# Batch 1's state exponentials transposed through memory and on VectorE instead of on TensorE, in a fused cross-attention and feed-forward kernel

## The chip, the cores and the metric

The kernel runs on one core of a Trainium2 chip. Its metric is the time of one execution on the device, in microseconds (us); the median of the runs shown is used. All data are 32-bit floats. "PE" is TensorE, "DVE" VectorE, "ACT" ScalarE, "SP" SyncE, whose queue issues nearly all of the DMAs here.

## The reference, cut to what matters

The input x is (B, H, S, D) = (8, 8, 512, 64), the state (8, 8, 32, 64). Tokens read the state and the state reads the tokens; the results of both, per batch 512 + 32 rows of 512 numbers, go through a feed-forward block.

```python
scores = scale * np.matmul(x, state.transpose(0, 1, 3, 2))
scores = scores - scores.max(-1, keepdims=True)
a = np.exp(scores)
a /= a.sum(-1, keepdims=True) + 1e-09
xread = np.matmul(a, state)
scores2 = scale * np.matmul(state, x.transpose(0, 1, 3, 2))
scores2 = scores2 - scores2.max(-1, keepdims=True)
a2 = np.exp(scores2)
a2 /= a2.sum(-1, keepdims=True) + 1e-09
sread = np.matmul(a2, x)
attn_out = np.concatenate([xread, sread], axis=2)
...
x = attn_out.transpose(0, 2, 1, 3).reshape(B * S, H * D)    # 4352 x 512
h = x @ w_in                                                # 512 x 2048
g = h * (1.0 / (1.0 + np.exp(-1.702 * h)))
return g @ w_out                                            # 2048 x 512
```

The weights come as 64-bit floats and are rounded to 32 bits on the chip.

## The kernel before, in words

The kernel is one program written out by hand: `tc.manual_schedule()` keeps each engine's instructions in the order of the source, and only the semaphores between engines are derived from which tile is read and written. So the place of a call in the source is its place in every queue that it touches, SP's included.

**Weights.** The 32 pieces of `PIECES` (16 of w_in, then 16 of w_out, one row block of 128 each) are loaded by `load_weight` (L199, 512 KB each) into rooms that are used in turn: a w_out piece i lies in the part i % 4 of the tile `later`, so its load waits until piece i - 4 has been rounded. Rounding a piece takes VectorE's mask (L221), then the clamp of its exponent (`round_a`), the fraction (L239), the sign (L245) and two combining steps (L258, L264). `round_a` puts the clamp on ScalarE as two activations (L232, L233), except for pieces 18 and 19 (`NFC * NPR + 2` and `+ 3`), where two VectorE instructions do it (L229, L230). `done["b"]` counts rounded pieces; `refill` issues loads after each; `rounds(n, ahead)` and `round_to` round further pieces, `powers_to(n)` does masks and clamps up to piece n.

**Batches 0 and 1** are treated first and together, while the weights arrive. Their token reads go through `M = w_in` times state (`att_M`) and then `up_x` or `up_late`, the hidden activations (PE at L655, the activation at L644, held back in a list and released by `gelus`). Their state reads go thus: `two_s_max` (L463), `two_s_exp` (eight exponentials over both batches at L474, into one tile `room`), `two_s_norm` (the inverse sums, L481 and L482), `att_eT` (L608 and L609), which turns the exponentials by 128 x 128 transposes on PE into PSUM and copies them on ScalarE to the tile `eT`, and `att_sread` (L622), 64 small matmuls of eT with the tokens, which lie with four neighbouring rows side by side.

**Batches 2 to 7** turn their exponentials otherwise: `att_s_exp` (L508) writes them in another order, `eT_out` (L588) writes them to the DRAM tile `squares` by four DMAs of 128 KB, `eT_in` (L594) reads that back as one DMA of 512 KB, and `eT_turn` (L598) transposes 32 x 32 blocks on VectorE, in place.

**Down projection of batch 0.** It is a seven-product scheme with sums of the operands (P1 to P7 in `pair`, L1539), run over eight pairs i of row blocks; for pair 0 the state reads of batches 1 and 0, `att_M(1, 2)`, `att_M(1, 3)` and an early `up_x` of batch 1 stand between P1 and P2. `left_sums` and `pair_sums` are the operand sums on VectorE (L1469). The order of the stretch in question is that of the source from `up_late(2 * nper + 1)` to the end of the branch `if i == 0` in the loop over HF.

Of the kernel before, what the change touches and what calls it, by code (L numbers as in the profile page):

```python
# [10 lines left out]
FP32 = mybir.dt.float32  # L11
I32 = mybir.dt.int32
U32 = mybir.dt.uint32
AF = mybir.ActivationFunctionType
# [6 lines left out]
def kernel(  # L21
# [36 lines left out]
    P = 128  # L58
# [157 lines left out]
    def mask(i):  # L216

        _, hi = words(i)
        sc = low[:, 2 + i % (AHEAD + 1)].bitcast(I32)
        power[i] = sc  # L220
        nc.vector.tensor_scalar(sc, hi, 0x7FF00000, None, ALU.bitwise_and)  # L221

    def round_a(i):

        if i not in power:
            mask(i)
        sc = power[i]
        if i in (NFC * NPR + 2, NFC * NPR + 3):
            nc.vector.tensor_scalar(sc, sc, most, least, ALU.min, ALU.max)  # L229
            nc.vector.tensor_scalar(sc, sc, -least, 8.0, ALU.add, ALU.mult)  # L230
            return
        nc.scalar.activation(out=sc.bitcast(FP32), in_=sc, func=AF.Relu, bias=edge[0], scale=-8.0)  # L232
        nc.scalar.activation(out=sc, in_=sc.bitcast(FP32), func=AF.Relu, bias=edge[1], scale=-1.0)  # L233
# [233 lines left out]
    def two_s_exp(b, room):  # L467
        a = A[b]
        sm = a["sm2"] = apool.tile([P, NG, 2], FP32, tag="sm4", name=f"sm4_{b}", bufs=2)
        a["e2"] = [(room[:, g], sm[:, g, :1]) for g in range(NG)]  # L470
        for g in range(NG):
            dst = room[:, g].rearrange("p (k i q) -> p k i q", k=2, i=2)
            for i in range(2):
                nc.scalar.activation(  # L474
                    out=dst[:, :, i], in_=a["s"][i][:, 2 * P * g : 2 * P * (g + 1)].rearrange("p (k q) -> p k q", k=2), func=AF.Exp,
                    bias=a["mx2"][:, 0, g : g + 1], scale=scale, accum_out=sm[:, g, i : i + 1],
                )

    def two_s_norm(b):
        sm = A[b]["sm2"]  # L480
        nc.vector.scalar_tensor_tensor(sm[:, :, 0], sm[:, :, 0], eps, sm[:, :, 1], ALU.add, ALU.add)  # L481
        nc.vector.reciprocal(out=sm[:, :, 0], in_=sm[:, :, 0])  # L482
# [12 lines left out]
    def att_s_exp(b, room=None):  # L495
        a = A[b]
        if room is None:
            room = e2_room[b] = apool.tile([P, NPR, S], FP32, tag="xT", name=f"e2_{b}")
        a["e2"] = []
        for g in range(NG):  # L500
            e = room[:, g]
            sm = apool.tile([P, 1], FP32, tag="sm2", name=f"sm2_{b}_{g}", bufs=4)
            out, src = e, a["s"][g]
            if b > 1:

                out = e.rearrange("p (i c a) -> p i a c", i=SCH, c=SCH)
                src = src.rearrange("p (i a c) -> p i a c", i=SCH, c=SCH)
            nc.scalar.activation(out=out, in_=src, func=AF.Exp, bias=a["mx2"][g], scale=scale, accum_out=sm)  # L508
            a["e2"].append((e, sm))
# [58 lines left out]
    def att_M(b, c, spare=False, banks=None, copied=True):  # L568

        m = mpool.tile([P, NG, FC], FP32, tag=f"M{turns['M'] % NFC if b < 2 else c}", name=f"M_{b}_{c}")  # L570
        turns["M"] += 1
        A[b]["M", c] = m
        name = f"M_{b}_{c}_"
        ps = banks or [
            psH.tile([P, FC], FP32, tag="h", name=name + str(g)) if spare else att_ps([P, FC], name + str(g)) for g in range(NG)
        ]
        by_state(b, ps, lambda rows, j: w_in[c][rows, j])
        M_banks[b, c] = ps
        if copied:
            M_copies(b, c)  # L580
# [3 lines left out]

    def eT_out(b):
        for j in range(NPR):
            src = e2_room[b][Ns * j : Ns * (j + 1), :NG].rearrange("n g (i q) -> n g i q", i=SCH)
            nc.sync.dma_start(squares[:, :, :, j].rearrange("i n g q -> n g i q"), src)  # L588

    def eT_in(b):  # L590

        a = A[b]
        a["eT"] = apool.tile([P, NG, SCH, P], FP32, tag="eT", name=f"eT_{b}")
        nc.sync.dma_start(a["eT"].rearrange("p g j q -> p (g j q)"), squares.rearrange("i n g j q -> (i n) (g j q)"))  # L594

    def eT_turn(b, g):
# [3 lines left out]
    def att_eT(b, g, spare=False):  # L600

        a = A[b]
        if g == 0:
            a["eT"] = apool.tile([P, NG, SCH, P], FP32, tag="e1" if b else "eT", name=f"eT_{b}")
        name = f"eT_{b}_{g}"
        ps = psH.tile([P, SCH, P], FP32, tag="h", name=name) if spare else att_ps([P, SCH, P], name)
        for c in range(SCH):
            nc.tensor.transpose(ps[:, c], a["e2"][g][0][:, P * c : P * (c + 1)], ident)  # L608
        nc.scalar.copy(a["eT"][:, g], ps)  # L609

    def att_sread(b):

        a = A[b]
        ps = att_ps([P, NG, D], f"sr_{b}")
        for g in range(NG):
            for c in range(SCH):
                for j in range(NPR):
                    st = slice(Ns * j, Ns * (j + 1))
                    e, v = a["eT"][:, g, c, st], xn[b][:, NG * j + g, c]
                    if b > 1:  # L620
                        e = a["eT"][:, g, j, Ns * c : Ns * (c + 1)]
                    nc.tensor.matmul(  # L622
                        ps[st, g], e, v,
                        start=(c == 0), stop=(c == SCH - 1),
                    )
        sr = apool.tile([P, P], FP32, tag="sr", name=f"sr_{b}", bufs=2)
        for g in range(NG):
            nc.scalar.activation(out=sr[:, D * g : D * (g + 1)], in_=ps[:, g], func=AF.Copy, scale=a["e2"][g][1])
        A[b]["sr"] = sr
# [11 lines left out]
    def gelus(n):  # L641
        for _ in range(n):
            fn, kw = waiting.pop(0)
            fn(**kw)  # L644
# [646 lines left out]
    def rounds(n, *ahead):  # L1291
        round_to(done["b"] + n, *ahead)
# [120 lines left out]
    def up_late(f, wait=True):  # L1413
        up_x(0, f, bank=late_banks[f - 2 * nper - 1], wait=wait)

    up_late(2 * nper + 1)
    att_M(0, 3)
    two_s_exp(1, room[:, NG:])
    two_s_max(0)
    up_late(2 * nper + 2)  # L1420
    two_s_exp(0, room[:, :NG])
    up_late(2 * nper + 3)
    up_late(3 * nper)
    rounds(3)
    for b in (1, 0):
        two_s_norm(b)
    up_late(3 * nper + 1)
    gelus(3)
    for g in range(NG):
        att_eT(1, g)  # L1430
    gelus(2)
    up_late(3 * nper + 2, False)
    up_late(3 * nper + 3, False)
    for g in range(NG):
        att_eT(0, g, True)


    B11, B12, B21, B22 = (w_out[:, HF * i : HF * (i + 1), HN * k : HN * (k + 1)] for i in range(2) for k in range(2))
# [22 lines left out]
    def pieces(t, *shape):  # L1461
        n, k = shape
        return t.rearrange("p a b -> p (a b)").rearrange("p (n k t) -> p n k t", n=n, k=k)
# [7 lines left out]
    def four(t):  # L1471
        return t.rearrange("p a b -> p (a b)").rearrange("p (n t) -> p n t", t=HS)
# [80 lines left out]
    for i in range(HF):  # L1553
        round_to(nin + 2 * i + 2)
        gelus(len(waiting))
        if i == 3:
            nc.scalar.copy(G[1, f_early // 2][:, f_early % 2], early)
        if i == 0:
            pair(i, "P1")
            att_sread(1)  # L1560
            att_M(1, 2, banks=bank_o[1::2])
            att_sread(0)
            att_M(1, 3, True)
            pair(i, "P2")
            f_early = rest.pop(0)
            early = xn[0].rearrange("p h c d -> p (h c d)")[:, :S]
            up_x(1, f_early, dst=early)
            att_srT(0)
            att_srT(1)
            t_room.append(pieces(apool.tile([P, NG, SCH * P], FP32, tag="eT", name="t_room_1"), 2, 2))  # L1570
            s_rooms.append(four(apool.tile([P, NG, NB * Ns], FP32, tag="e1", name="s4_room")))
            pair_sums(i)
            round_to(nin + 4)
            powers_to(nin + 6)
            pair(i, "P6")
            ps7["P7"], ps7["P3"] = (psH.tile([P, FC], FP32, tag="h", name=f"down_{k}") for k in (7, 3))
            ps7["P4"], up_bank = (att_ps([P, FC], f"down_{k}") for k in (4, "up"))
        else:
            pair_sums(i)
            pair(i, "P1", "P2")  # L1580
        if i == 2:
            G[1, f_early // 2] = free.pop(0)
        if i > 1 and i % 2 == 0:
            up_x(1, rest.pop(0), bank=up_bank, wait=True)
        if i == HF - 1:
            k1 = s_rooms[0][:, :2]
            nc.scalar.copy(k1, ps7["P1"].rearrange("p (r n) -> p r n", r=2))
        late()
        if i > 1 and i % 2:
            up_x(1, rest.pop(0), bank=up_bank if i < HF - 1 else bank_o[0], wait=True)  # L1590
        if i == HF // 2 + 1:
            load_state(2)
            load_x_squares(2)
# [140 lines left out]
```

## Time and profile before

| | |
|---|---|
| median of three runs | 689.23 us (688.90 to 689.25) |
| the profiled execution | 688.99 us, of which the span from first to last instruction is 687.2 |
| granted TensorE clock, mean | 0.998 |
| PE busy | 677.6 us, 5355 matmuls |
| DVE busy | 558.0 us, 1066 instructions |
| ACT busy | 327.9 us, 725 instructions |
| transposes of batches 0 and 1 on PE (L608) | 16 matmuls, 2.1 us |
| block transposes on DVE (L598) | 12, median 702 ns |
| DMAs on SP's queue (q1) | 86.40 MB, 42.6% of 16 engines' span |

The profile is of one execution. Its page gives busy times, the chain of work that ended last (followed back from the last instruction), the costliest groups and the DMA issues. The trace behind it gives, for any stretch, a timeline of each engine with start and length of each instruction in us, and in brackets how long the engine was idle before it and what it waited for. The ends of matmuls are modelled and overlap their successors; distances between starts tell the pace.

### The profile page before, as it was taken

Reading aid. Unit: us, or ns where it says so; the run is one execution under the profiler, and the core shown is the slowest. Engines: PE = TensorE matmul, PEld = TensorE weight load, DVE = VectorE, ACT = ScalarE, POOL = GpSimd, SP = SyncE. Lnnn points to the kernel's source line nnn. Section 1 sums busy time; section 2 is a strip of 40 time slices with the busy share of each in tenths; the row PEclk is TensorE's granted clock in tenths of the full one; section 3 lists DMA queues with packets and bytes.
Section 4 is the critical chain, followed back from the end, with each engine's and each line's share of the span. In section 5 each row is a group of like instructions: output and inputs, shape, how many; then the busy total and the mean of one; then the engine's idle time right before and its main releaser. Section 6 shows DMA issues by size and latency. Waiting matters only on the chain.

```text
span 687.2 us, 13616 instructions
## 1 busy us (share of the span) xinstructions
PE 677.6 (99%) x5355; PEld 578.7 (84%) x5355; DVE 558.0 (81%) x1066; ACT 327.9 (48%) x725; POOL 1.5 (0%) x10
## 2 busy tenths in 40 slices
PE   8999999999999999999999999999999999999996
PEld 4443687769989999889988998899988998999995
DVE  6999899999998886988878796888698885986540
ACT  7799744134355533752375335544375237421410
POOL 0000000000000000000000000000000000000000
PEclk9999999999999999999999999999999999999999
DMA  9731245338262764156443745176415640251000
GB/s 318 302 105 49 93 140 147 116 119 270 89 156 78 208 192 113 32 166 190 151 67 112 205 144 113 32 208 192 115 27 170 187 152 1 77 169 47 2 3 29
DMA packets 100159, 87.39 MB, mean 127 GB/s; under 512 B 56576, under 2 KB 79616, under 8 KB 100096
## 3 DMA queue, kind: packets, MB, share of 16 engines
q1 hardware_dynamic: 99552, 86.40, 42.6%
q8 instruction: 42, 0.69, 0.4%
q10 hardware_dynamic: 544, 0.13, 0.1%
q14 instruction: 21, 0.17, 0.1%
HBM read 68.94 MB, written 17.56 MB: 126 GB/s over the span
## 4 chain that ended last, share of the span: by engine, by line
PE 94%; DMA 2%; DVE 2%; ACT 1%; issue 0%; DVEq 0%; ACTq 0%
PE low L802 28%; PE o L1212 15%; PE o L802 15%; PE upx L1212 6%; PE o L1539 4%; PE M L430 4%; PE down L1539 3%; PE o L655 3%; PE h L655 3%; PE o L701 3%; PE upw L1212 2%; PE o L851 2%; PE down_up L655 1%; PE o L430 1%; PE sr L622 1%; PE upx_sr L1212 1%
## 5 line engine op out<-in xcount | busy, mean ns | idle before, releaser
L802 PE MATMUL low<-w_out,g_room 128*128 128x128 f32 x416 | 54.3, 276 | 0.0
L802 PEld LDWEIGHTS low<-w_out,g_room 128*128 128x128 f32 x416 | 50.5, 192 | 4.5 <-issue 4.2
L1212 PE MATMUL o<-ta,M 128*128 128x256 f32 x192 | 49.9, 382 | 0.0
L1212 PE MATMUL upx<-aT,M 128*128 128x256 f32 x192 | 49.4, 380 | 0.0
L802 PE MATMUL low<-low,g_room 128*128 128x128 f32 x336 | 43.3, 275 | 0.0
L1212 PEld LDWEIGHTS o<-ta,M 128*128 128x128 f32 x192 | 35.5, 190 | 6.0 <-ACT g_room L1258 1.6
L802 PEld LDWEIGHTS low<-low,g_room 128*128 128x128 f32 x336 | 40.3, 192 | 0.0
L1212 PEld LDWEIGHTS upx<-aT,M 128*128 128x128 f32 x192 | 36.0, 190 | 4.8
L1218 ACT ACTIVATE g_room<-o 128x512 f32<-128x512 f32 (+1 forms) x56 | 31.4, 560 | 10.7 <-PE o L1212 10.7
L802 PE MATMUL low<-sums,later 128*128 128x128 f32 x272 | 34.9, 275 | 0.0
L566 ACT COPY M<-M 128x512 f32<-128x512 f32 x53 | 27.5, 596 | 15.2 <-PE M L430 15.2
L802 PEld LDWEIGHTS low<-sums,later 128*128 128x128 f32 x272 | 32.7, 192 | 0.1
L858 DVE TENSOR_TENSOR g_room<-g_room 128x512 f32<-128x512 f32 x48 | 31.8, 686 | 0.2
L1212 PE MATMUL o<-ta,ms 128*128 128x256 f32 x120 | 30.8, 379 | 0.0
L232 ACT ACTIVATE low<-low,edge 128x512 f32<-128x512 int32 x30 | 21.8, 726 | 17.6 <-DVE low L221 17.6
L1258 ACT COPY g_room<-o 128x512 f32<-128x512 f32 (+1 forms) x28 | 15.6, 556 | 25.0 <-PE o L1212 25.0
L1218 ACT ACTIVATE g_room<-g_room 128x512 f32<-128x512 f32 (+1 forms) x28 | 16.8, 602 | 20.8 <-DVE g_room L1221 20.8
L1212 PEld LDWEIGHTS o<-ta,ms 128*128 128x128 f32 x120 | 22.8, 190 | 3.1
L1212 PE MATMUL o<-aT,m 128*128 128x256 f32 x96 | 24.6, 379 | 0.0
L802 PEld LDWEIGHTS o<-w_out,g_room 128*128 128x128 f32 x160 | 19.4, 192 | 5.0 <-issue 5.0
L430 PE MATMUL M<-w_in,stT 64*32 64x512 f32 x344 | 23.2, 592 | 0.0
L858 DVE TENSOR_TENSOR g_room<-g_room,later 128x512 f32<-128x512 f32 x35 | 22.8, 685 | 0.0
(321 smaller groups left out, 1640.8 us busy)
## 6 DMA issues: line engine op xcount, KB each, us to landing
low<-low SPq DMA_DIRECT2D x108, 256.0 KB, 2.6
low<-low SPq DMA_DIRECT2D x11, 768.0 KB, 4.5
later<-in_moe_w_out_dram SPq DMA_DIRECT2D x16, 512.0 KB, 3.4
w_out<-in_moe_w_in_dram SPq DMA_DIRECT2D x12, 512.0 KB, 10.0
xsq<-in_x_dram SPq DMA_DIRECT2D x96, 64.0 KB, 2.3
xn<-in_x_dram SPq DMA_DIRECT2D x12, 512.0 KB, 4.2
out_dram<-osb SPq DMA_DIRECT2D x15, 256.0 KB, 2.2
out_dram<-later SPq DMA_DIRECT2D x14, 256.0 KB, 2.2
```

Of the source, the lines that this page charges most:

```text
L232: nc.scalar.activation(out=sc.bitcast(FP32), in_=sc, func=AF.Relu, bias=edge[0], scale=-8.0)
L430: nc.tensor.matmul(ps[g][st], state_of(b, NG * j + g, g), rhs(rows, j), start=True, stop=True)
L566: nc.scalar.copy(A[b]["M", c][:, g], ps)
L655: nc.tensor.matmul(hps, lhs[i], rhs[i], start=(i == 0), stop=(i == n - 1))
L701: nc.tensor.matmul(ps[:, r], lhs[f][:, P * r : P * (r + 1)], rhs[:, f], start=(first and r == 0 and f == 0), stop=(f == HF - 1), skip_grou ...
L802: nc.tensor.matmul(ps, lhs[f], rhs[:, f], start=(first and f == 0), stop=(f == QF - 1), skip_group_check=True)
L851: nc.tensor.matmul(ps[:, r], lhs[f][:, P * r : P * (r + 1)], rhs[:, f], start=(r == 0 and f == 0), stop=(f == HF - 1), skip_group_check=True,)
L858: nc.vector.tensor_tensor(out=out, in0=x0, in1=x1, op=op)
L1212: nc.tensor.matmul(ps[:, k], lhs[i][:, o : o + P], rhs[i], start=(first and k == 0 and i == 0), stop=(i == n - 1), skip_group_check=True,)
L1218: nc.scalar.activation(out=dst, in_=src, func=AF.Gelu_apprx_sigmoid)
L1258: nc.scalar.copy(c12, Y(u))
L1539: nc.tensor.matmul(ps7[name][:, HN * r : HN * (r + 1)], lhs[:, P * r : P * (r + 1)], rhs, start=(i == 0 and r == 0), stop=(i == HF - 1), s ...
```

## The change

Batch 1's exponentials no longer pass through PE. `two_s_exp` writes them, for batch 1 only, in runs of 32 in another order (the sums and values are the same); `eT_out(1)` follows it at once; `eT_in(1)` stands after the next rounded piece; and two `eT_turn(1, g)` stand on VectorE after the norms, in place of `att_eT(1, g)`. `att_sread` takes batch 1's exponentials in the squares' order. Piece 19 of the weights is clamped on ScalarE, its mask placed ahead of the block transposes and its clamp (`powers_to(nin + 4)`) behind batch 0's `att_eT`. In the branch for pair 0, `pair_sums`, the rounding of piece 19 and with it the clamp of piece 20 are called ahead of P2 and of the early `up_x`; the two rooms for their sums are taken there too. Batch 0 keeps its transposes on PE.

```diff
-        if i in (NFC * NPR + 2, NFC * NPR + 3):
+        if i == NFC * NPR + 2:
             nc.vector.tensor_scalar(sc, sc, most, least, ALU.min, ALU.max)
...
         for g in range(NG):
-            dst = room[:, g].rearrange("p (k i q) -> p k i q", k=2, i=2)
+            if b:
+                dst = room[:, g].rearrange("p (v k i a) -> p i k v a", v=SCH, k=2, i=2)
+                view = lambda t: t.rearrange("p (k v a) -> p k v a", k=2, v=SCH)
+            else:
+                dst = room[:, g].rearrange("p (k i q) -> p i k q", k=2, i=2)
+                view = lambda t: t.rearrange("p (k q) -> p k q", k=2)
             for i in range(2):
                 nc.scalar.activation(
-                    out=dst[:, :, i], in_=a["s"][i][:, 2 * P * g : 2 * P * (g + 1)].rearrange("p (k q) -> p k q", k=2), func=AF.Exp,
+                    out=dst[:, i], in_=view(a["s"][i][:, 2 * P * g : 2 * P * (g + 1)]), func=AF.Exp,
...
-            src = e2_room[b][Ns * j : Ns * (j + 1), :NG].rearrange("n g (i q) -> n g i q", i=SCH)
+            src = e2_room[b][Ns * j : Ns * (j + 1)].rearrange("n g (i q) -> n g i q", i=SCH)
...
-        a["eT"] = apool.tile([P, NG, SCH, P], FP32, tag="eT", name=f"eT_{b}")
+        a["eT"] = apool.tile([P, NG, SCH, P], FP32, tag="e1" if b == 1 else "eT", name=f"eT_{b}")
         nc.sync.dma_start(a["eT"].rearrange("p g j q -> p (g j q)"), squares.rearrange("i n g j q -> (i n) (g j q)"))
...
-                    if b > 1:
+                    if b:
                         e = a["eT"][:, g, j, Ns * c : Ns * (c + 1)]
...
-    two_s_exp(1, room[:, NG:])
+    e2_room[1] = room[:, NG:]
+    two_s_exp(1, e2_room[1])
+    eT_out(1)
     two_s_max(0)
...
-    rounds(3)
+    rounds(1, 1)
+    eT_in(1)
+    rounds(1, 1)
+    rounds(1, 0)
     for b in (1, 0):
         two_s_norm(b)
+    mask(nin + 3)
+    for g in range(NG):
+        eT_turn(1, g)
     up_late(3 * nper + 1)
-    gelus(3)
-    for g in range(NG):
-        att_eT(1, g)
-    gelus(2)
+    gelus(5)
     up_late(3 * nper + 2, False)
     up_late(3 * nper + 3, False)
     for g in range(NG):
         att_eT(0, g, True)
+    powers_to(nin + 4)
...
             att_M(1, 3, True)
+            t_room.append(pieces(apool.tile([P, NG, SCH * P], FP32, tag="eT", name="t_room_1"), 2, 2))
+            s_rooms.append(four(apool.tile([P, NG, NB * Ns], FP32, tag="e1", name="s4_room")))
+            pair_sums(i)
+            round_to(nin + 4, 1)
             pair(i, "P2")
             f_early = rest.pop(0)
             early = xn[0].rearrange("p h c d -> p (h c d)")[:, :S]
             up_x(1, f_early, dst=early)
             att_srT(0)
             att_srT(1)
-            t_room.append(pieces(apool.tile([P, NG, SCH * P], FP32, tag="eT", name="t_room_1"), 2, 2))
-            s_rooms.append(four(apool.tile([P, NG, NB * Ns], FP32, tag="e1", name="s4_room")))
-            pair_sums(i)
-            round_to(nin + 4)
             powers_to(nin + 6)
```

More of the change, by code (lines that the diff above doesn't have):

```diff
@@ L497, in att_s_exp @@
         if room is None:
-            room = e2_room[b] = apool.tile([P, NPR, S], FP32, tag="xT", name=f"e2_{b}")
+            room = apool.tile([P, NPR, S], FP32, tag="xT", name=f"e2_{b}")
+            e2_room[b] = room[:, :NG]
         a["e2"] = []
@@ L603, in att_eT @@
         if g == 0:
-            a["eT"] = apool.tile([P, NG, SCH, P], FP32, tag="e1" if b else "eT", name=f"eT_{b}")
+            a["eT"] = apool.tile([P, NG, SCH, P], FP32, tag="eT", name=f"eT_{b}")
         name = f"eT_{b}_{g}"
```

## The prediction

> **What bounds the kernel now.** I read the page's first and fourth parts, then the list of PE's waits, then the timelines of the stretch that the change touches (62 to 84 us), engine by engine.
>
> ```profile
> PE 677.6 (99%) x5355; PEld 578.7 (84%) x5355; DVE 558.0 (81%) x1066; ACT 327.9 (48%) x725; POOL 1.5 (0%) x10
> ...
> PE 94%; DMA 2%; DVE 2%; ACT 1%; issue 0%; DVEq 0%; ACTq 0%
> ```
>
> PE is busy 99% of the span and holds 94% of the chain that ended last. The whole list of PE's waits has six rows, of which the longest is
>
> ```profile
> PE warm L131 <- DVE one L123: 1.2, 1, 1.2
> ```
>
> The six sum to 3.6 us, and the timeline puts all of them in the first 14 us; between 60 and 140 us the same list is empty. So whatever is taken from or added to PE's queue after 14 us should reach the end one for one: no later PE wait is there to swallow it. PE around the change (start, length, line, tile):
>
> ```profile
> 68.51 1.04 PE L608 MATMUL eT<-ident,e 128*128 128x128 f32 x8
> 69.38 3.60 PE L655 MATMUL o<-aT,M 128*128 128x512 f32 x8
> 72.82 1.04 PE L608 MATMUL eT<-ident,e 128*128 128x128 f32 x8
> 73.69 1.03 PE L1539 MATMUL o<-w_out,g_room 128*128 128x256 f32 x4
> 74.65 1.10 PE L622 MATMUL sr<-sums,eT 128*32 128x64 f32 x64
> 75.68 1.09 PE L430 MATMUL o<-w_in,two 64*32 64x512 f32 x16
> ```
>
> Lengths overlap (ends are modelled); the distance between starts is the price: 69.38 - 68.51 = 0.87 us for batch 1's eight transposes, 0.87 for the product P1, 1.03 for batch 1's state read. VectorE and ScalarE in the same stretch:
>
> ```profile
> 65.97 0.19 ACT L474 ACTIVATION_READ_ACCUMULATOR e<-sums,mx 128x1 f32 x1
> 70.06 0.42 DVE L221 TENSOR_SCALAR low<-later 128x512 int32<-128x512 int32 x1
> 70.52 0.43 DVE L229 TENSOR_SCALAR low<-low 128x512 int32<-128x512 int32 x1
> 70.98 0.43 DVE L230 TENSOR_SCALAR low<-low 128x512 int32<-128x512 int32 x1
> 73.40 0.69 DVE L1469 TENSOR_TENSOR s_room<-g_room,sums 128x512 f32<-128x512 f32 x1
> 83.97 0.69 DVE L245 SCALAR_TENSOR_TENSOR low<-later,low 128x512 int32<-128x512 int32 x1 [1.92 <-ACT low L233]
> ```
>
> Batch 1's exponentials are complete at 65.97 + 0.19 = 66.16. VectorE is nearly full up to 82.05, then idles 1.92 us for ScalarE's half of a weight piece. The path through memory is already used by batches 2 to 7; the SP queue at batch 2, and the issue-to-landing times (issues by line; the last number of each) read
>
> ```profile
> 158.52 2.70 SPq L588 DMA_DIRECT2D squares<-e  x4
> ...
> later<-in_moe_w_out_dram SPq DMA_DIRECT2D x16, 512.0 KB, 3.4
> squares<-e SPq DMA_DIRECT2D x24, 128.0 KB, 2.6
> eT<-squares SPq DMA_DIRECT2D x6, 512.0 KB, 7.2
> ```
>
> One write issue holds SP for 2.70 / 4 = 0.67 us; a write lands 2.6 us after its issue. A 512 KB load lands after 3.4 us where the queue is empty (weights), after 7.2 where several other transfers stand around it (batch 2's eT).
>
> [...] in the changed order SP does hold the read for all four writes, so the two latencies add. [...] L508 writes single floats 128 bytes apart and takes 1182 ns for 512 elements. [...]
>
> **The change part by part.**
>
> 1. Removed from PE: eight transposes, 0.87 us. All of it lies on the path: -0.87. Without other waits P1 starts at 72.82 and batch 1's state read at 74.65 - 0.87 = 73.78. In their way is only the bank of up_late(15), last read by the activation that ends near 70.05; PE now comes to it at 69.38 + 1.72 - 0.87 = 70.23. The margin is 0.18 us; I cost it at nothing.
>
> 2. ScalarE's exponentials write runs of 32 floats instead of 128. [...] I take 0.50 us as before. Bounds: 0 and, at L508's rate (about twice per element), 4 x 0.41 = 1.6 us more. Two of four eT copies vanish (1.1 us) and piece 19's two clamps come (1.41, L232 and L233 from start to start at 82.43); the sum is +0.3 us on an engine busy 48%. The clamps start after batch 0's eT copies, about 73.9, and end by 75.3; VectorE wants them after 79. Nothing on the path.
>
> 3. VectorE loses two clamps (L229, L230), and piece 19's mask moves behind the norms: piece 18 comes sooner by 71.33 - 70.06 = 1.27 us. The norms, 0.53 us long, begin at 72.87 - 1.27 = 71.60 and end at 72.13; the moved mask (0.34) ends at 72.47. Added: two block transposes, 0.70 us each in this trace (L598), 0.62 from start to start.
>
> 4. The SP queue, which decides. The four writes follow the exponentials: issues from about 66.2, the fourth at 66.2 + 3 x 0.67 = 68.2, SP free at 68.9. The load of piece 20 (before: 65.24) follows at 69.0. The read of eT waits for the last write: 68.2 + 2.6 = 70.8[...]: 70.95. It lands at 70.95 + 3.45 = 74.4, with piece 20's load mostly through. Behind it pieces 21 and 22 go at about 71.3 and 71.6 (before: 68.64, 72.04) and land near 76; their masks come after 80. Piece 23 waits on VectorE as before. None of these loads is late.
>
> 5. The new wait. VectorE is at the first eT transpose at 72.47 and stands until 74.45. Transpose 0 runs to 75.15, transpose 1 from 75.07 to 75.77. PE's state read, ready at 73.78, needs half 0 (75.20, so 1.4 us of idle PE) and half 1: 75.82 + 0.51 = 76.33. In the trace of before the next row starts at 75.68. Sum on PE: 76.33 - 75.68 = +0.65, that is -0.87 removed and +1.52 of wait.
>
> 6. Behind VectorE's wait stand the sums of the left side, of pair 0, the rounding of piece 19 and pair 1's sums; PE's products wait for them. All start at 75.69 instead of 73.40: +2.29. The sum for P6 of pair 0 ends at 76.85 + 2.29 = 79.14; PE comes to P6 at 81.66 + 0.65 = 82.31. Piece 19: 80.12 + 2.29 = 82.41, wanted by P1 of pair 1 at 86.62. Pair 1's sums end at 82.05 + 2.29 = 84.34, wanted at 88.3. So 3 to 4 us of cover, each worth its excess if it went. Moving piece 20's clamps ahead of the early activation removes the 1.92 us idle at 83.97: VectorE resumes with piece 20 at about 84.3, only 0.4 behind before, with PE 0.65 behind. No further wait.
>
> Sum: 688.99 (profiled execution: span 687.2 and 1.8 around it) + 0.65 = 689.6. The median shown is 689.23, 0.24 above that execution; carried to it, 689.9.
>
> **Rivals.**
>
> *In time.* The memory path ends before PE asks: the read must land by 73.0. Then the whole 0.87 is won: 688.4. It would need the write and the read together in 6.8 us from 66.2, of which issues take 2.0 and latencies 2.6 + 3.45. Only a read shorter by 1.4 us than any weight load does it; a partial gain needs a landing before 73.75. Chance 0.09.
>
> *The read is crowded (slower).* Piece 20's 512 KB go 2 us before the eT read, pieces 21 and 22 right behind it, and the writes' 512-byte rows fill the queue before. Batch 2's eT read stood in such company and took 7.2 us. At that price it lands at 78.1 and PE ends 4.3 us late: 693.6. Each 0.1 us of later landing costs 0.1; slower by over 0.2% (1.4 us) begins at a landing of about 75.15, only 0.75 past my value, so this rival decides early. Against it: in batch 2 over 1 MB stood ahead of the read, here half of that, mostly gone. Likeliest in this case: landing at 76, 691.5. Chance 0.29.
>
> *The exponentials scatter (slower).* With 1.6 us more on ScalarE the writes start later by as much: 689.9 + 1.6 = 691.5. Chance 0.04. *VectorE's shift breaks the cover* (a late sum at P6 or later): at least 0.7 us past my forecast, about 691. Chance 0.03, as 3 us would have to be missing.
>
> *Forecast*: 0.55.
>
> **How the numbers follow.** What a measurement of this kernel can tell from no change is about 0.2%, 1.4 us. Forecast and in-time cases lie within it, except that a low scatter on the full gain could pass it: faster 0.02. Slower: 0.29 + 0.04 + 0.03 less a part that stays under 1.4 us: 0.35. Same: 0.63. The range runs from the full gain, 688.4, up to a read landing near 76.5, 692.0; beyond lie the far part of the crowded case and about 0.02 below.
>
> **What would show it.** Eight fewer PE transposes at 68.5; a PE wait of about 1.4 us at the batch 1 state read, released by VectorE's transpose, that in turn waited about 2 us for the eT read. Four write issues from 66.2, the read at about 70.95. No VectorE idle near 84. I am wrong if PE shows no wait (landing by 73), if the exponentials take over 0.6 us each, if the read's latency is far from 3.45, or if a second PE wait appears between 76 and 100 us.

## The result and the profile after

The changed kernel takes 692.37 us (median of six runs, 691.95 to 694.63) against 689.22 us before (median of six runs as well, 688.90 to 689.82); the ratio is 1.0053 (95% interval 1.0037 to 1.0070). It is slower by some 3 us, above the forecast's 689.9 and just above its range. The profiled execution took 692.53 us, with a span of 690.7 (before 687.2), at a mean clock of 0.996 (before 0.998). Two of the six runs took 694.20 and 694.63 us, at a mean clock of 0.994; no trace shows where their further 2 us went. In the trace of after everything ahead of the new wait lies about 0.1 us later than in that of before: P1 begins at 72.93 instead of 73.69 - 0.87 = 72.82.

The page of after: busy times, and the chain that ended last by engine.

```profile
PE 678.7 (98%) x5347; PEld 578.6 (84%) x5347; DVE 558.0 (81%) x1066; ACT 328.0 (47%) x725; POOL 1.5 (0%) x10
...
PE 89%; DMA 4%; ACT 3%; DVE 3%; SPq 0%; issue 0%; DVEq 0%; ACTq 0%
```

Eight matmuls fewer, and yet PE is busy for longer: 678.7 us instead of 677.6. A wait alone would add to the span and leave the busy time smaller; something made the remaining matmuls longer. The chain's share on DMA has doubled, from 2% to 4%. The list of PE's waits in after has one new row, at its head (us in total, times, longest):

```profile
PE sr L629 <- DVE eT L605: 2.8, 1, 2.8
```

PE's timeline around it (start, length, line, tiles, and in brackets the idle time before and its releaser):

```profile
72.06 1.04 PE L615 MATMUL eT<-ident,e 128*128 128x128 f32 x8
72.93 1.03 PE L1552 MATMUL o<-w_out,g_room 128*128 128x256 f32 x4
76.75 1.54 PE L629 MATMUL sr<-sums,eT 128*32 128x64 f32 x64 [2.79 <-DVE eT L605]
78.22 1.96 PE L430 MATMUL o<-w_in,two 64*32 64x512 f32 x16
80.11 1.43 PE L629 MATMUL sr<-xn,eT 128*32 128x64 f32 x64
81.47 1.09 PE L430 MATMUL M<-w_in,two 64*32 64x512 f32 x16
82.49 1.13 PE L1552 MATMUL o<-w_out,sums 128*128 128x256 f32 x4
```

Two things are to be seen. PE waits 2.79 us for batch 1's exponentials, twice the forecast's 1.4. And from start to start the four groups after the wait take 1.47, 1.89, 1.36 and 1.02 us: the first and third are state reads that took 1.03 before, the second a product that took 1.02 (the fourth, of the same kind, still does). From 76.75 to 82.49 is 5.74 us where before it was 4.10 (74.65 to 78.75): 1.64 us are lost while PE works. The table by stretches of after has the reason. Its columns are the stretch and its length, then busy time and number of instructions of PE, of PE's weight loads, of VectorE, ScalarE and GpSimd, then the clock granted to TensorE (1.00 is full speed), the busy share of the DMA engines and the GB/s that they moved:

```profile
70.00:73.00 3.00, 3.00 (x15) 1.80 (x14) 2.58 (x9) 3.00 (x8) 0.00 (x0) 1.00 0.77 236
73.00:76.70 3.70, 0.96 (x5) 0.51 (x4) 0.77 (x2) 2.37 (x5) 0.00 (x0) 1.00 0.97 375
76.70:77.40 0.70, 0.65 (x40) 0.63 (x44) 0.70 (x2) 0.00 (x0) 0.00 (x0) 1.00 0.21 82
77.40:80.90 3.50, 3.50 (x81) 1.67 (x83) 3.36 (x8) 1.15 (x4) 0.00 (x0) 0.51 0.03 12
80.90:84.00 3.10, 3.10 (x66) 1.81 (x59) 3.10 (x8) 2.31 (x6) 0.00 (x0) 1.00 0.13 20
```

For 3.5 us after the wait TensorE's granted clock is half. The same table of before shows 1.00 in all these stretches; two of its rows:

```profile
73.00:76.70 3.70, 3.70 (x92) 2.39 (x90) 3.53 (x10) 2.46 (x6) 0.00 (x0) 1.00 0.38 142
77.40:80.90 3.50, 3.50 (x53) 1.84 (x43) 3.47 (x9) 2.07 (x6) 0.00 (x0) 1.00 0.18 44
```

In stretches of 0.1 us the half clock of after lies from 77.45 to 80.86, that is 3.41 us. The row from 73.00 shows the other thing: while PE waits, the DMA engines are 97% busy and move 375 GB/s (before: 38%, 142 GB/s).

How the wait came about, in after's timelines of SP's queue (SPq) and VectorE, and in the window's DMA issues (the last number is from issue to landing):

```profile
66.29 2.69 SPq L595 DMA_DIRECT2D squares<-e  x4
69.08 0.56 SPq L199 DMA_DIRECT2D later<-in_moe_w_out_dram  x1
71.15 0.34 SPq L601 DMA_DIRECT2D eT<-squares  x1
71.58 0.86 SPq L199 DMA_DIRECT2D later<-in_moe_w_out_dram  x2
```

```profile
72.25 0.40 DVE L221 TENSOR_SCALAR low<-later 128x512 int32<-128x512 int32 x1
75.93 1.30 DVE L605 STREAM_TRANSPOSE eT<-eT 128x512 f32<-128x512 f32 x2 [3.29 <-DMA eT<-squares]
```

```profile
eT<-squares SPq DMA_DIRECT2D x1, 512.0 KB, 4.7
```

The read is issued at 71.15, as forecast (70.95 and the 0.1 of offset), and lands at 75.84, 4.69 us later, where 3.45 was forecast. VectorE reaches the transposes at 72.6 and stands until 75.93; PE's state read starts at 76.75, when the first of the two transposes is done.

The sum on PE closes: -0.87 removed, +2.79 of wait, +1.64 of half clock is +3.56; the product P2 starts at 82.49 instead of 78.75, +3.74, less 0.11 of offset: +3.63. The spans differ by 3.5.

### The profile page after: what moved, and what is told of

Read it like the earlier page. It is cut to its first block, busy times and chain, and to the rows that moved or that the text cites. A ratio compares the mean times of both kernels' runs of the same rounds, so it can differ in the third digit from the quotient of the medians.

```text
span 690.7 us, 13608 instructions
## 1 busy us (share of the span) xinstructions
PE 678.7 (98%) x5347; PEld 578.6 (84%) x5347; DVE 558.0 (81%) x1066; ACT 328.0 (47%) x725; POOL 1.5 (0%) x10
## 4 chain that ended last, share of the span: by engine, by line
PE 89%; DMA 4%; ACT 3%; DVE 3%; SPq 0%; issue 0%; DVEq 0%; ACTq 0%
PE low L809 28%; PE o L1219 15%; PE o L809 15%; PE upx L1219 6%; PE o L1552 4%; PE M L430 3%; PE down L1552 3%; PE o L708 3%; PE upw L1219 2%; PE o L858 2%; PE down_up L662 1%; PE o L430 1%; PE sr L629 1%; PE h L662 1%; PE upx_sr L1219 1%; ACT low L233 1%
## 5 line engine op out<-in xcount | busy, mean ns | idle before, releaser
L233 ACT ACTIVATE low<-low,edge 128x512 int32<-128x512 f32 x31 | 22.4, 722 | 1.1
```

## The experiments

My theory after the result had two parts: the half clock is a consequence of PE's idle time and costs 1.6 us by itself; and the read is late because piece 20's load stands ahead of it and loads 21 and 22 behind it. Rivals: that the state read is slow for another cause than the clock (its new layout of eT, or VectorE's work); that the second part of the change (clamps, order) costs the time; and that only one of the neighbours makes the read late.

**PE kept busy during the wait.** Three matmuls of 128 x 512 whose result nobody reads stand between P1 and the state read, in a bank that is free. Nothing is left out.

```diff
             pair(i, "P1")
+            for _ in range(3):
+                nc.tensor.matmul(bank_o[1], ident, w_in[0][:, 0], start=True, stop=True)
             att_sread(1)
```

> The changed kernel with three matmuls of the identity with a piece of w_in (128x512, 0.86 us each by the trace, results overwritten) put on PE between P1 and batch 1's state read, where PE stood idle for 2.8 us. Theory of the clock: the records of the changed kernel show a granted clock of 0.5 for 3.4 us after the idle; with 2.6 of the 2.8 us filled, the half clock does not come, the three groups after the wait take 1.03 us each again instead of 1.47, 1.89 and 1.36, and the time falls by about 1.6 us to 690.7 although nothing waits any less. Rival (those groups are slow because VectorE, ScalarE and the DMAs compete with them, or because of their operands' new layout): they stay slow and the time stays at 692.4.

Measured: 691.54 us (690.51 to 692.41, five runs), ratio 1.0035 (1.0021 to 1.0049). PE in the profiled execution:

```profile
73.84 2.74 PE L1574 MATMUL o<-w_in,ident 128*128 128x512 f32 x6
77.28 1.20 PE L629 MATMUL sr<-sums,eT 128*32 128x64 f32 x64 [0.69 <-DVE eT L605]
78.41 1.09 PE L430 MATMUL o<-w_in,two 64*32 64x512 f32 x16
79.42 1.10 PE L629 MATMUL sr<-xn,eT 128*32 128x64 f32 x64
80.46 1.09 PE L430 MATMUL M<-w_in,two 64*32 64x512 f32 x16
```

With useless work in the gap the groups are back at 1.13, 1.01 and 1.04 us, with the same layout of eT and the same VectorE work beside them. The granted clock is 1.00 from 70 to 84 us. In this execution the read happened to take 5.27 us, 0.58 more than in after, and still the kernel was 0.99 us shorter than after's profiled one; 0.99 and 0.58 together are about the clock's 1.64. (The expected 690.7 is missed by 0.8 us, most of it this later read, which the expectation took as unchanged.) The five runs have mean clocks of 0.998 to 1.000, the six of after 0.994 to 0.996. So the half clock is what made PE slow, and it followed from the idle time.

**The load ahead of the writes.** `eT_out(1)` moves behind the first rounded piece, so that piece 20's load goes first and nothing stands between writes and read.

```diff
     two_s_exp(1, e2_room[1])
-    eT_out(1)
     two_s_max(0)
...
     rounds(1, 1)
+    eT_out(1)
     eT_in(1)
```

> The changed kernel with the four writes of the exponentials issued behind the load of weight piece 20 instead of ahead of it, so that this load is issued near 65.3 us and not between the writes and the read of eT. Theory of the crowded queue: the read (4.69 us from issue to landing in the changed kernel, 3.4 for a weight load of the same size alone) was held up by piece 20's 512 KB; issued still at about 71.1, it lands at 74.6, PE's wait falls by 1.2 us to about 1.6, no half clock follows, and the time is 689.4 to 689.7. Rival (a read of what has just been written to memory takes 4.7 us by itself): the landing stays near 75.8 and the time at 692.4. Against both: if the load ahead delays the writes, the read is issued later, and the gain is smaller.

Measured: 690.62 us (689.49 to 692.44, 20 runs), ratio 1.0018 (1.0012 to 1.0025). SP and PE in the profiled execution, which was the shortest of the twenty:

```profile
65.23 0.33 SPq L199 DMA_DIRECT2D later<-in_moe_w_out_dram  x1
66.19 2.85 SPq L595 DMA_DIRECT2D squares<-e  x4
71.06 0.35 SPq L601 DMA_DIRECT2D eT<-squares  x1
```

```profile
75.25 1.20 PE L629 MATMUL sr<-sums,eT 128*32 128x64 f32 x64 [1.40 <-DVE eT L605]
76.38 1.09 PE L430 MATMUL o<-w_in,two 64*32 64x512 f32 x16
...
79.45 1.13 PE L1552 MATMUL o<-w_out,sums 128*128 128x256 f32 x4
```

```profile
eT<-squares SPq DMA_DIRECT2D x1, 512.0 KB, 3.3
```

The writes start at about the same time as in after (66.29), for the exponentials set that. The read takes 3.28 us, PE waits 1.40, the clock stays at 1.00, and P2 starts 0.70 after before's. That is the forecast's own sum (+0.65), found in a kernel that differs from the changed one by one moved call. But only a few of the twenty executions come near the expected 689.4 to 689.7; the median is 0.9 us above it.

**The same kernel, profiled in another execution.**

> The load-first kernel looked at again, for the landing of the eT read in another execution. If its spread comes from the landing, then time and landing move together: a run that is 1 us longer than 689.5 shows a read that lands 1 us later than 74.34 and a PE wait of 2.4 us. If the landing is 74.3 again with a longer time, the cause is elsewhere, and the trace shows where.

Measured: 691.96 us, one run, clock 0.995. Its issues, VectorE and the clock by stretches:

```profile
eT<-squares SPq DMA_DIRECT2D x1, 512.0 KB, 4.1
```

```profile
75.48 1.30 DVE L605 STREAM_TRANSPOSE eT<-eT 128x512 f32<-128x512 f32 x2 [2.80 <-DMA eT<-squares]
```

```profile
75.00:76.00 1.00, 0.00 (x0) 0.00 (x0) 0.52 (x1) 0.44 (x1) 0.00 (x0) 1.00 1.05 426
76.00:77.00 1.00, 0.70 (x28) 0.73 (x32) 1.00 (x3) 0.00 (x0) 0.00 (x0) 0.56 0.93 377
77.00:78.00 1.00, 1.00 (x48) 0.99 (x39) 0.90 (x2) 0.00 (x0) 0.00 (x0) 0.50 0.22 86
```

The read of the very same program took 4.09 us this time, PE waited 2.30 instead of 1.40, and the half clock came, again for 3.41 us. Landing and time move together, as the first of the two expectations had it, and behind the wait of 2.30 us the clock adds its part: from the state read to P2 it takes 5.57 us, against 4.20 in the first profile. In the twenty runs above, 18 have a clock of 0.998 to 1.000 and take 689.49 to 691.17 us; the two longest (691.47 and 692.44) have 0.996. So the spread of that kernel has two parts: landings that differ between executions, and in the latest of them the clock.

**The second part of the change alone.** Batch 1 goes through PE as before; only piece 19's clamp on ScalarE and the earlier sums and rounding in the branch for pair 0 remain. The diff is against the kernel before.

```diff
-        if i in (NFC * NPR + 2, NFC * NPR + 3):
+        if i == NFC * NPR + 2:
...
+            pair_sums(i)
+            round_to(nin + 4, 1)
             pair(i, "P2")
```

> The second half of the change alone: batch 1's exponentials are transposed on PE as before, but piece 19 is clamped on ScalarE, and the sums of pair 0, piece 19 and the clamp of piece 20 stand ahead of P2. Theory (the loss is all of the memory path): 689.2, within 0.1% of the kernel before, with no new PE wait; VectorE's idle near 84 us shrinks from 1.9 to under 0.5. Rival (moving the clamps costs by itself): 690 or more, with a PE wait between 76 and 100 us.

Measured: 689.37 us (688.77 to 689.91, 12 runs), ratio 1.0001 (0.9993 to 1.0010), no new PE wait, as expected. That part neither costs nor brings anything that can be measured; the 3 us are the memory path's.

**The state read further back on PE.** `att_sread(1)` moves behind `att_M(1, 3)`, so that 3.1 us of other products can cover the read; SP's order is that of the changed kernel.

```diff
             pair(i, "P1")
-            att_sread(1)
             att_M(1, 2, banks=bank_o[1::2])
             att_sread(0)
             att_M(1, 3, True)
+            att_sread(1)
```

> The changed kernel with batch 1's state read moved on PE behind the two state products of batch 1 and batch 0's state read (about 3.1 us of work that needs nothing of it), everything else as changed. Theory (what was lost is PE standing in order behind a late read, plus the clock): PE reaches the read at about 76.95, the block transposes end at 76.65 and 77.25, so PE waits under 0.3 us there, no half clock, and most of the 0.87 us of removed transposes is won: 688.4 to 688.8. Rival (VectorE, 3.8 us behind after its wait, is what is late): PE waits at P6 instead, whose sum ends near 80.9 when PE comes at 80.9; each further 0.1 us late costs 0.1, 689 to 690.

Measured: 690.25 us (689.49 to 691.02, 20 runs), ratio 1.0015 (1.0009 to 1.0022). PE's waits in the profiled execution (690.87 us):

```profile
PE sr L629 <- DVE eT L605: 0.8, 1, 0.8
PE down L1552 <- ACT xn L651: 0.7, 1, 0.7
```

The expected 688.4 to 688.8 is missed. The read took 5.96 us here, so a wait of 0.84 us stays even behind 3.1 us of cover. The second wait is the forecast's rival of the broken cover, at a place that it did not name: VectorE resumes 1.1 us later than in after and makes piece 20's mask late; ScalarE stands 3.72 us for it with the clamp, until 83.32, and the early activation that PE's products need is queued behind that clamp.

**The loads behind the read held back, in two ways.** Loads 21 and 22 wait until VectorE has turned the blocks. In the first pair a DMA of 128 x 4 bytes, written after the block transposes, keeps them back on SP: once in the load-first order (the read stands alone), once in the changed kernel's order (piece 20's load still ahead).

```diff
-        while done["b"] > NPR and done["load"] < len(PIECES) and before(done["load"]) < done["b"]:
+        while not held_back and done["b"] > NPR and done["load"] < len(PIECES) and before(done["load"]) < done["b"]:
...
     eT_in(1)
+    held_back.append(1)
...
         eT_turn(1, g)
+    nc.vector.memset(flag, 0.0)
+    nc.sync.dma_start(flag_out, flag)
+    held_back.clear()
+    refill()
```

> As e2_load_first (piece 20's load ahead of the writes), and the loads of pieces 21 and 22 held on SP until VectorE has done both block transposes (a 512-byte DMA of a flag that VectorE sets then stands in front of them; one VectorE memset is added). So the read of eT has the DMA queue to itself. Theory of the crowded queue: e2's profiled run, with a landing after 3.28 us, was its fastest of 20 (689.49, median 690.62), so the loads behind still hurt in most runs; alone, the read lands after 3.3 to 3.5 us in every run, PE waits 1.4 us, no half clock, and the median is 689.6 to 690.0, with a smaller spread. Rival (the spread is of the read itself, or of the writes): median and spread stay as e2's, 690.6.

> The changed kernel with only the loads of pieces 21 and 22 held back, by the same flag; piece 20's load stays between the writes and the read. It parts what stands ahead of the read from what stands behind it. If the load ahead is the main cause, the read's 4.7 to 6.0 us fall little (4.2 or more), PE still waits over 2.2 us, the half clock comes in most runs, and the median is 691.3 to 692.4. If the loads behind are, the read lands after 3.5 us or so and the median is 690.0 to 690.6. If both share it, about 691.

Measured, five runs each: 693.88 us (ratio 1.0066, 1.0052 to 1.0080) and 695.48 us (1.0086, 1.0073 to 1.0099), both longer than the changed kernel and than either expectation. As totals they say nothing of the read, because the hold brought a cost of its own, as VectorE in the load-first variant shows:

```profile
87.57 0.43 DVE L221 TENSOR_SCALAR low<-later 128x512 int32<-128x512 int32 x1 [5.62 <-DMA later<-in_moe_w_out_dram]
```

Load 21, issued at 75.80 behind the small write, was there only at 87.5. In the other run of the pair VectorE waited 5.2 us for the same load, and the DMA engines moved 98, 16, 4 and 74 GB/s in the four microseconds from 78 us, and 31 from 82 to 86. What the pair does tell is the read: from its issue to VectorE's start 3.33 us when it is alone, 4.54 with the load ahead.

In the second pair a two-column VectorE copy out of the loads' rooms takes the small DMA's place, so that the loads wait for that copy; the diff is against the first pair.

```diff
+    nc.vector.tensor_copy(touched, later[:, 2:5:2, 0].bitcast(I32))
-    nc.vector.memset(flag, 0.0)
-    nc.sync.dma_start(flag_out, flag)
```

> The order in which piece 20's load goes ahead of the four writes, and loads 21 and 22 wait on SP for a two-column VectorE copy that stands behind the block transposes (no flag transfer). The read stands alone: it should land 3.3 us after its issue, loads 21 and 22 be issued near 75.5 and land near 79, long before VectorE masks piece 21 near 87, so no late wait. Theory A (in the load-first kernel without this hold the spread of times comes from loads 21 and 22, which share the transfer engines with the read): 689.9, and the spread of the runs shrinks to about that of the kernel before, 1 us. Theory B (the spread comes from piece 20's load or from the writes, so that the hold changes nothing): median 690.5 and a spread of 2 us or more as without the hold.

> The changed kernel, with loads 21 and 22 held in the same way, but piece 20's load still between the writes and the read. Theory A (the load that stands ahead makes the read late): latency about 4.5 us as in the run with the flag transfer, PE waits 2.4 us, the clock stays at 1.0 in most executions, time 691.0 (before + 0.65 + 1.05). Theory B (the loads behind it make it late): latency 3.4, PE waits 1.4, 689.9.

Measured, load-first order: 689.77 us (688.63 to 691.79, 12 runs), ratio 1.0006 (0.9997 to 1.0015). In the profiled execution, the shortest of the twelve, the read took 3.25 us, PE waited 1.1, and VectorE waited for no load although these were issued at 75.14 and 75.53; so it was the small DMA that had made them late. The median came down to theory A's value, but the spread did not: 3.2 us, and the two longest runs (691.38 and 691.79) again have a clock of 0.996. Theory A is only half right: the loads behind are not all of what makes the landing differ. The intervals of the two load-first kernels overlap a little, so the gain by the hold is likely and not settled.

Changed kernel's order: 691.82 us (691.00 to 692.18, six runs), ratio 1.0033 (1.0021 to 1.0046). The read took 4.44 us with nothing behind it and PE waited 2.38: theory A's mechanism. The reads of the two orders in the profile's rounding, first the load-first order's:

```profile
eT<-squares SPq DMA_DIRECT2D x1, 512.0 KB, 3.3
eT<-squares SPq DMA_DIRECT2D x1, 512.0 KB, 4.4
```

Theory A's 691.0 is missed, because I took the clock to hold at 2.4 us. In the changed order it does not:

```profile
76.00:77.00 1.00, 0.84 (x52) 0.81 (x56) 1.00 (x4) 0.00 (x0) 0.00 (x0) 1.00 0.00 0
77.00:78.00 1.00, 1.00 (x36) 0.43 (x32) 0.90 (x2) 0.52 (x2) 0.00 (x0) 0.60 0.36 74
78.00:79.00 1.00, 1.00 (x16) 0.00 (x0) 1.00 (x4) 0.00 (x0) 0.00 (x0) 0.50 0.89 315
```

From the state read to P2 it takes 5.74 us, 1.64 more than before, just as in after. In the variant with the small DMA the same wait of 2.38 us left the clock at 1.00.

All latencies of the 512 KB read, one execution each (us from issue to landing; * to VectorE's start, about 0.1 more):

| | loads 21, 22 behind | nothing behind |
|---|---|---|
| piece 20's load ahead | 4.69, 5.27, 5.96 | 4.44, 4.54* |
| nothing ahead | 3.28, 3.24, 4.09 | 3.25, 3.33* |

With nothing behind, the load ahead costs 1.2 us, in both pairs. The loads behind add from nothing to 1.5 us, differently in each execution. The 3.28 and the 3.25 are of the shortest executions of their kernels. The traces also show what stood in the read's way. The four writes and piece 20's load are 1.05 MB together. From 64.7 us to 71.1, about where the read is issued, the DMA engines moved 105 GB/s in after, 0.67 MB: some 0.38 MB of the load was still to come. In the load-first kernel (first profile) they moved 166 GB/s, 1.06 MB: nothing was left.

**All of it reordered.** The load-first order; on PE the state read of batch 1 behind both att_M and batch 0's read; on VectorE the three sums of the left side ahead of the block transposes; and piece 20's clamp behind the early activation.

```diff
-    for g in range(NG):
-        eT_turn(1, g)
...
-            att_sread(1)
             att_M(1, 2, banks=bank_o[1::2])
             att_sread(0)
             att_M(1, 3, True)
+            turns_of(left_sums(i)[:3])
+            for g in range(NG):
+                eT_turn(1, g)
+            att_sread(1)
...
-            round_to(nin + 4, 1)
+            round_to(nin + 4, 0)
```

> A version meant to beat both kernels: piece 20's load ahead of the writes as in e2; batch 1's state read on PE behind the two state products of batch 1 and batch 0's read as in e4; on VectorE the three sums of the left side ahead of the block transposes; the clamp of piece 20 behind the early activation again (in e4 that order cost PE 0.7 us). Theory (the transposes were worth their 0.87 us, all that was lost was queueing): block transposes done by 76.8 even with a landing at 75.4, PE at the read at 76.75, no PE wait over 0.2 us from 20 us on, no half clock, 688.3 to 688.6. Rival (a landing later than 75.5 in most runs, as e2's median suggests): waits of up to 1 us at the read or at P6 remain, 688.8 to 689.3, no gain that can be told from the kernel before.

Measured: 688.43 us (688.17 to 688.81, 21 runs) against 689.24 beside it; ratio 0.9987 (0.9981 to 0.9994). It is shorter than both kernels. VectorE and PE:

```profile
74.07 0.69 DVE L1480 TENSOR_TENSOR g_room<-g_room 128x512 f32<-128x512 f32 x1
74.83 1.30 DVE L605 STREAM_TRANSPOSE eT<-eT 128x512 f32<-128x512 f32 x2
77.78 0.42 DVE L1480 TENSOR_TENSOR sums<-w_out 128x256 f32<-128x256 f32 x1 [1.64 <-PE sr L629]
```

```profile
76.05 1.09 PE L430 MATMUL M<-w_in,two 64*32 64x512 f32 x16
77.07 1.10 PE L629 MATMUL sr<-sums,eT 128*32 128x64 f32 x64
78.10 1.13 PE L1548 MATMUL o<-w_out,sums 128*128 128x256 f32 x4
```

No bracket stands on PE's rows or on the transposes: neither waits for the read any more. The read landed at 74.81, just as VectorE got there, and PE comes to the state read at 77.07, about 1 us after the second half is turned. VectorE now waits 1.64 us for PE's state read instead, ahead of its next sum, but no PE wait follows from that. The gain, 0.81 us, is about the removed transposes' 0.87. The runs spread over 0.6 us instead of 3, all at mean clocks of 0.998 to 1.000: with slack behind the landing its scatter seems no longer to reach PE, nor does the clock fall. The new order with the transposes left on PE was not run; PE had no wait in this stretch before that such an order could have removed.

## Why the prediction was wrong, point by point

- *What bounds the kernel* was right: no PE wait later swallowed anything. All that was added at 76 us reached the end: 3.6 us at P2, 3.5 in the span.
- *Step 1* (eight transposes, -0.87) was right; the reordered kernel won 0.81. *Step 2* was right: batch 1's exponentials take 0.49 us each, and the second part of the change alone is neutral; the rival of the scatter is out (its bound came from L508, whose 1182 ns stand beside 581 for L644's activation of the same 128 x 512 in the trace of before). *Step 3* was right within 0.1 us (VectorE at the transposes at 72.6; two take 1.30). *Step 6* held in after (no later PE wait, no VectorE idle near 84), though the kernel with the later state read shows the margin's end: 1.1 us more and ScalarE's queue gave PE a wait of 0.7.
- *Step 4 failed in one term*, the read's latency. The issue time was right: in after the read was issued 0.07 us behind the last write's landing at 71.08, where the sum to 70.95 has 0.15, an estimate of mine. The 3.45 us are the price of a read that stands alone (3.25 measured so), and I wrote that piece 20's load would be mostly through. It was not, some 0.38 of its 0.52 MB were still to come, and the latency was 4.69 in after. Of the 1.24 us missing, the load ahead makes 1.2 by the runs with nothing behind (4.44 against 3.25). The median row of other loads, 3.4, is no price in a queue with a load just ahead.
- *Step 5 failed by a term that was not there.* It counted a wait as its length. After 2.79 us of idle PE the clock was halved for 3.41 us, at 1.64 us. The forecast's 1.4 us brought no half clock where PE waited just that long (1.40 in the load-first kernel, at a clock of 1.00), and I did not ask what the crowded case's longer wait would do to the clock. All three traces that show a half clock show it for 3.41 us. PE was not idle throughout an equal stretch ahead of the fall: in those 3.41 us it idled for 2.72 in after, 2.37 in the changed order with the loads held by the copy, 2.12 in the second profile of the load-first kernel.
- *The sum*: 0.65 + 1.24 + 1.64 = +3.53; the spans of the two profiled executions differ by 3.5, the medians by 3.15.
- *The rivals.* "The read is crowded" was the case that came true, and I gave it 0.29. Its likeliest landing, 76, is close to the measured 75.84. The writes, too, filled the DMA engines, as it said: from 67.7 to 69.0 us, before piece 20's load was issued, they kept them 97% busy at 178 GB/s. Its rule, 0.1 us for each 0.1 us of later landing, gives 689.6 + 1.44 = 691.0 for the profiled execution, which took 692.53; the missing 1.5 us are the clock again, which bends the rule upwards: behind three of the four waits of 2.30 to 2.79 us it fell, behind 1.40 it did not. For the same reason the range's upper end was wrong: 692.0 stood for a landing near 76.5, and 75.84 was enough to pass it.
- *Forecast against rival*: the evidence that I weighed, "half of that, mostly gone", compared amounts of data that had been queued. What decided is how much of it was still to move when the read was issued, and the order of the calls sets that.

What stays open: how much idling in which position brings the half clock (2.12 and 2.37 us of a 3.41 us stretch did, a wait of 2.38 in another execution did not, and no run shows what made the difference), why the read of one and the same program takes 3.28 or 4.09 us, and what the two longest runs of the changed kernel spent their further 2 us on.

## What to carry to other kernels

Price a DMA on the path by what is still queued when it is issued. The lone transfer's latency of 3.25 us did not hold here with a 512 KB load just ahead (4.44), and moving the writes behind that load was worth 1.2 us of it; loads just behind added up to 1.5 us too. Price a long PE wait with the clock's term: here, of the four profiled executions with a wait of 2.30 to 2.79 us, three lost 1.4 to 1.6 us more to a half clock. When a short piece of PE work goes to a longer path through memory, put enough other work ahead of its consumers, on PE and on VectorE, to cover the latest landing and not only the usual one. Of the kernels here only the one that did so won the transposes' time.

## What the runs showed of the hardware that was not expected

- The clock was half for 3.41 us after 2.12 to 2.72 us of idling in the 3.41 us ahead of its fall (three traces); behind a wait of 2.38 us in a fourth trace it stayed at 1.00. In no trace did a wait of 1.40 us or less at that place bring it, and with filler matmuls in the gap it did not come.
- A DMA of 128 x 4 bytes ahead of a 512 KB load: that load, issued at 75.80, held VectorE until 87.57. With the small DMA replaced by a VectorE copy, loads issued at 75.14 and 75.53 made nobody wait. Why the small DMA did this is not shown.
- The latency of one 512 KB read with two loads behind it differed between kernels and executions from 3.2 to 4.1 us, in one program from 3.28 to 4.09, and with one ahead as well from 4.7 to 6.0.
